# Attention, soft MoE and Mish MLP on one core: the attention order written out for all five queues, the values' products in two blocks a pair

## The chip, the cores and the metric

The kernel runs on 1 core of one Trainium2 chip. The metric is the device time of one execution in microseconds. The engines are TensorE (PE; its weight loads are listed as PEld), VectorE (DVE), ScalarE (ACT), GpSimd (POOL) and SyncE (SP); here SP issues every DMA transfer. A queue of an engine runs its instructions strictly in the order in which they were put there.

## The reference

Three layers in a row, all inputs float32 but the last layer's weights, which are float64 and are converted on the chip.

```python
def _attn_ref(q, k, v):                       # 4 batches, 8 heads, 576 rows, 64 wide
    q_rot, k_rot = rotate(q), rotate(k)       # rotary embedding
    scores = q_rot @ k_rot.T / sqrt(64)
    attn = exp(scores - max(scores)); attn /= sum(attn) + 1e-9
    return attn @ v

def _moe_ref(x, phi, w1, w2):                 # x: 2304 x 512, 32 slots, 8 experts
    logits = x @ phi
    d = softmax over rows (axis 0); c = softmax over slots (axis 1)
    slot_input = d.T @ x
    slot_out = per expert: relu(slot_input @ w1) @ w2
    return c @ slot_out

def _moe2_ref(x, w_in, w_out):                # 512 -> 2048 -> 512
    h = x @ w_in
    return (h * tanh(softplus(h))) @ w_out
```

## The kernel before, in words

**Attention** works on 16 pairs of heads (`p` = 0 to 15, four pairs a batch). Each of q and k is loaded (`load_pair`), rotated on POOL (`rope_pair`, four tensor operations in `rotate`, L228 to L236), transposed on PE (`f_main`, L285) and split into a high and a low part (ACT L290, DVE L294). Twelve SBUF-to-SBUF transfers (`stack`, L317) lay the parts of both heads out so that three float32r products can stand for one float32 product. The last 64 rows of each head are a remainder and go through `load_rem`, `rope_rem` and `f_rem` once a batch or pair.

A pair has nine score tiles (`S`): four of 128 query rows for each head and one (`s_mm2`, L353) for both heads' remainder rows. Each tile is 4 matmuls of 288 columns (8 in the ninth). `M` is its maximum on DVE (L361), `E` its exponential on ACT (L367). `T`, `K` and `R` transpose the probabilities on PE (L374, L388, L394, L396) and copy them to SBUF (`evac`, L410 or L413, on ACT or DVE by a table or by load counters). `V` (`av(p, 0, c)`, 256 columns) and `W` (`av(p, 1, c)`, 320 columns) multiply them with the values (L429): for each of five blocks of keys `c` one matmul per head, the two heads in the two halves of the array's columns, accumulated in one PSUM tile. Each such matmul is two records in the trace. `X` (`xback`) transposes the result back (L449, L451), takes the routing logits (L455, L457) and scales both by the softmax sums. After every fourth pair a batch goes through five units `m_lt`, `m_cols`, `m_disp`, `m_slots`, `m_rows` (action `F`).

Beside this, 20 pieces of the float64 weights are converted in attention (action `C`: `cv_more`, `cv_act` L500 and L501 on ACT, `cv_bits` L506 to L508 on DVE, `cv_sum` L512 and L513 on POOL, then a store to a scratch in DRAM), and 1 MB weight tiles of the MoE layer are fetched into a ring (`fetch`).

**What sets the order.** `PLAN` is a list of nine steps of one pair, and the loop over `p` emits the actions in that order. The emitted order is a priority: the scheduler that places the instructions on the queues moves them by its own estimate of when each is ready, and only instructions passed to `tc.keep_in_program_order` keep their place among each other. Before, these are the weight fetches, the loads of the first two pairs and the warm-up matmuls. So the five blocks of `V` and of `W`, and the two heads in one block, can be parted by other PE work.

PSUM has eight banks: two tiles of two banks for scores (`ps_s`), three of one bank for everything else (`ps_m`) and one for the values' products (`ps_a`).

**After attention** (from `m_sit`, L778) come the experts (`h_ps` L834, `so_ps` L900), which read the ring of weight tiles, and the Mish MLP (`hp` L1004, `o_ps` L1038), which is most of the time from 440 us on.

Of the kernel before, what the change touches and what calls it, by code (L numbers as in the profile page):

```python
# [7 lines left out]
F32 = mybir.dt.float32  # L8
# [13 lines left out]
QA, QAR, QZ, QBR, QB, KC, QKW = 0, 512, 576, 640, 704, 1216, 2432  # L22
# [15 lines left out]

EVAC = {"T3": "d", "T4": "d", "K1": "a", "T0": "a", "T5": "a", "T2": "a"}
# [3 lines left out]
def kernel(  # L43
# [30 lines left out]
    ps_m = psx.enter_context(tc.tile_pool(name="ps_m", bufs=3, space=PSUM))  # L74
    ps_a = psx.enter_context(tc.tile_pool(name="ps_a", bufs=1, space=PSUM))
# [105 lines left out]
    load = {"a": 0.0, "d": 0.0}  # L181
# [73 lines left out]
    part = {}  # L255

    def f_rem(p):
        if p >= NP:
            return
        b, hp = divmod(p, H // 2)  # L260
        ps = ps_m.tile([128, 2, 1, R], F32, tag="m", name="m_rem")
        nc.tensor.transpose(ps.rearrange("p a o r -> p (a o r)"), rem[b][:, hp * 128:(hp + 1) * 128], ident)
        for x in "hl":
            part[x, p] = ae.tile([128, 2, 640], F32R, tag="part" + x, name="part" + x)
        src = ps.to_broadcast([128, 2, 2, R])
        hi, lo = (part[x, p].rearrange("p a (o r) -> p a o r", r=R)[:, :, 0:10:9, :] for x in "hl")

        def act():
            nc.scalar.copy(hi, src)
            load["a"] += 270  # L270

        def dve():
            nc.vector.tensor_tensor(out=lo, in0=src, in1=hi.bitcast(F32), op=ALU.subtract)
            load["d"] += 330

        act_q.append(act)
        dve_q.append(dve)

    def f_main(p, nm):
        if p >= NP:  # L280
            return
        ps = ps_m.tile([128, 512], F32, tag="m", name="m_" + nm)
        t = rope.pop((nm, p))
        for c in range(4):
            nc.tensor.transpose(ps[:, c * 128:(c + 1) * 128], t[:, c, :], ident)  # L285
        i, scale = ("qk".index(nm), SCALE if nm == "q" else 1.0)
        hi, lo = (part[x, p][:, i, R:R + 512] for x in "hl")

        def act():
            nc.scalar.activation(out=hi, in_=ps, func=AF.Copy, scale=scale)  # L290
            load["a"] += 480

        def dve():
            nc.vector.scalar_tensor_tensor(out=lo, in0=ps, scalar=scale, in1=hi.bitcast(F32),  # L294
                                           op0=ALU.mult, op1=ALU.subtract)
            load["d"] += 600
            if p:
                for h in range(2):
                    stack(p, nm, h)

        act_q.append(act)
        dve_q.append(dve)

    def stack(p, nm, h):

        st, s2 = qk_st[p % 2], k2_st[p % 2]
        for x, o in (("h", 0), ("l", 64)):
            t = part[x, p][64 * h:64 * h + 64]
            if nm == "q":
                c = (QA, QBR)[h]  # L310
                todo = [(st[o:o + 64, c:c + S], t[:, 0, R - h * R:][:, 0:S])]
# [3 lines left out]
            for out, in_ in todo:  # L315
                if p or h:
                    nc.sync.dma_start(out=out.bitcast(F32), in_=in_.bitcast(F32))  # L317
                else:

                    (nc.vector.tensor_copy if o else nc.scalar.copy)(out, in_)  # L320

    act_q = []
    dve_q = []

    def flush(lst):
        while lst:
            lst.pop(0)()

    def s_mm(p, s, qc, h, first, last):
        st = qk_st[p % 2]  # L330
        for half in range(2):
            o = h * S + half * 288
            nc.tensor.matmul(s[:, half, 0:288], lhsT=st[:, qc:qc + 128], rhs=st[:, KC + o:KC + o + 288],  # L333
                             start=first, stop=False)
            nc.tensor.matmul(s[:, half, 0:288], lhsT=st[:, qc:qc + 128], rhs=k2_st[p % 2][:, o:o + 288],  # L335
                             start=False, stop=last)

    def s_tile(p, t, h):

        s = ps_s.tile([128, 2, 512], F32, tag="s", name="s")  # L340
        if t < 4:
            s_mm(p, s, (QA, QB)[h] + t * 128, h, True, True)
        else:
            s_mm2(p, s)
        return s

    def s_mm2(p, s):
        st = qk_st[p % 2]
        for half in range(2):
            n = 0  # L350
            for o, qc in ((half * 288, QAR), (KB + half * 288, QZ)):
                for rhs in (st[:, KC + o:KC + o + 288], k2_st[p % 2][:, o:o + 288]):
                    nc.tensor.matmul(s[:, half, 0:288], lhsT=st[:, qc:qc + 128], rhs=rhs,  # L353
# [800 lines left out]
```

## Time and profile before

| | us |
|---|---|
| median of 3 runs | 674.24 |
| lowest and highest of them | 671.77, 676.41 |
| span of the profiled execution | 670.1 |
| first score matmul in it | 19.33 |
| remainder tile (L353) of pair 1 and of pair 15 | 59.64, 378.50 |
| `m_sit`, first work after attention | 397.35 |

The span runs from the first to the last instruction; the median also holds what lies around it, 4.1 us here. Busy time of PE is the union of its instructions with modelled ends, so the chain of waits is used for the length of a single piece.

### The profile page before, as it was taken

To read this page: it belongs to the slowest core of one execution; us is meant where nothing else is said; L and a number is where in the kernel's file an instruction comes from. 1 tells how busy PE (TensorE), PEld (TensorE's weight loads), DVE (VectorE), ACT (ScalarE), POOL (GpSimd) and SP (SyncE) were. 2 spreads that over 40 slices of the span, in tenths; PEclk is the share of its full clock that TensorE was granted. 3 is DMA by queue.
4 is the path that set the end of the run, shared out by engine and by line. 5 is a ranking of instruction groups with operands and counts; after the bars stand their busy time and mean duration, and the time that the engine had idled before them with its cause. 6 is when DMAs were issued, how large, how long until landed. Compare 5 with 4: busy or idle time off the path is not lost.

```text
span 670.1 us, 11089 instructions
## 1 busy us (share of the span) xinstructions
PE 625.2 (93%) x4022; PEld 461.3 (69%) x4022; DVE 406.5 (61%) x824; ACT 336.4 (50%) x757; POOL 218.2 (33%) x263
## 2 busy tenths in 40 slices
PE   1598999989899999999999998999999999999997
PEld 1475677666577767777667653377787888888885
DVE  5777888786686866565756533177876533353342
ACT  2566776684776556665656411167765312222121
POOL 5758869755858644345400010000000000000000
PEclk9999999999999999999999999999999999999999
DMA  9678689868786965346359499962400200030004
GB/s 259 160 187 236 187 268 273 231 212 237 161 266 218 264 184 166 103 128 189 81 176 302 158 338 324 389 262 95 156 33 31 64 1 0 1 95 0 1 1 94
DMA packets 59607, 109.43 MB, mean 163 GB/s; under 512 B 12832, under 2 KB 25248, under 8 KB 59040
## 3 DMA queue, kind: packets, MB, share of 16 engines
q1 hardware_dynamic: 59552, 108.72, 54.2%
q8 instruction: 32, 0.52, 0.3%
q14 instruction: 23, 0.19, 0.1%
HBM read 70.25 MB, written 9.96 MB: 120 GB/s over the span
## 4 chain that ended last, share of the span: by engine, by line
PE 77%; DMA 9%; DVE 7%; ACT 2%; POOL 2%; issue 2%; SPq 1%; DVEq 0%; ACTq 0%; POOLq 0%
PE o_ps L1038 29%; PE m_av L429 13%; PE t L374 7%; PE s L333 5%; PE s L335 4%; PE hp L1004 3%; PE s L353 2%; DMA w<-in_moe_w_in_dram 2%; PE so_ps L900 2%; DMA w<-in_moe_w_dram 2%; DVE nmax L361 1%; PE m_lg L455 1%; PE tk L388 1%; PE m_k L285 1%; DMA w<-in_moe_w_out_dram 1%
## 5 line engine op out<-in xcount | busy, mean ns | idle before, releaser
L361 DVE TENSOR_REDUCE nmax<-s 128x1 f32<-128x576 f32 x144 | 108.0, 753 | 64.3 <-PE s L335 39.5
L367 ACT ACTIVATE P<-s,nmax 128x576 f32<-128x576 f32 x144 | 107.2, 745 | 36.3 <-DVE nmax L361 25.5
L1038 PE MATMUL o_ps<-wo_l,gh 128*128 128x512 f32 x288 | 112.9, 392 | 0.0
L1038 PE MATMUL o_ps<-wo_h,gh 128*128 128x512 f32 x288 | 112.9, 392 | 0.0
L1038 PE MATMUL o_ps<-wo_h,gl 128*128 128x512 f32 x288 | 100.7, 390 | 0.9 <-DVE gl L1019 0.9
L1011 ACT ACTIVATE room<-hp 128x512 f32<-128x512 f32 x72 | 43.0, 599 | 106.7 <-PE hp L1004 102.2
L333 PE MATMUL s<-qk_st 128*128 128x288 f32 x256 | 85.6, 349 | 10.3 <-ACT P L367 5.2
L374 PE MATMUL t<-cs,P 128*128 128x128 f32 x512 | 79.0, 282 | 4.8 <-ACT P L367 2.7
L410 ACT COPY PT<-t 128x512 f32<-128x512 f32 x92 | 53.5, 586 | 49.8 <-PE t L374 49.2
L429 PE MATMUL m_av<-PT,w 128*64 128x320 f32 (+1 forms) x384 | 73.3, 421 | 1.9 <-ACT PT L399 1.3
L374 PEld LDWEIGHTS t<-cs,P 128*128 128x128 f32 x512 | 59.6, 143 | 21.8 <-issue 9.7
L335 PE MATMUL s<-k_st,qk_st 128*128 128x288 f32 x256 | 73.8, 302 | 0.0
L333 PEld LDWEIGHTS s<-qk_st 128*128 128x128 f32 x256 | 49.9, 195 | 29.5 <-ACT P L367 9.1
L1013 DVE CAST gh<-room 128x512 fp32r<-128x512 f32 x49 | 20.9, 427 | 79.4 <-ACT room L1011 79.3
L1038 PEld LDWEIGHTS o_ps<-wo_h,gl 128*128 128x128 f32 x288 | 53.9, 188 | 13.2 <-DVE gl L1019 1.7
L231 POOL TENSOR_TENSOR w<-w,cs 128x512 f32<-128x512 f32 x34 | 45.2, 1332 | 54.1 <-PE m_k L285 46.6
L1038 PEld LDWEIGHTS o_ps<-wo_h,gh 128*128 128x128 f32 x288 | 54.1, 188 | 9.4
L1038 PEld LDWEIGHTS o_ps<-wo_l,gh 128*128 128x128 f32 x288 | 54.3, 189 | 9.0 <-DVE wo_l L891 0.2
L1019 DVE TENSOR_TENSOR gl<-room,gh 128x512 fp32r<-128x512 f32 x72 | 49.6, 691 | 4.6
L335 PEld LDWEIGHTS s<-k_st,qk_st 128*128 128x128 f32 x256 | 50.2, 196 | 0.0
L228 POOL TENSOR_TENSOR w<-w,cs 128x512 f32<-128x512 f32 x34 | 45.7, 1345 | 8.6 <-DMA w<-in_q_dram 2.9
L429 PEld LDWEIGHTS m_av<-PT,w 128*64 128x64 f32 x384 | 26.5, 136 | 23.0 <-issue 9.2
(175 smaller groups left out, 1011.5 us busy)
## 6 DMA issues: line engine op xcount, KB each, us to landing
w<-in_moe_w_dram SPq DMA_DIRECT2D x28, 1024.0 KB, 7.1
w<-in_moe_w_in_dram SPq DMA_DIRECT2D x16, 512.0 KB, 7.3
qk_st<-parth SPq DMA_DIRECT2D x46, 144.0 KB, 3.2
qk_st<-partl SPq DMA_DIRECT2D x46, 144.0 KB, 3.2
room<-in_moe_w_out_dram SPq DMA_DIRECT2D x12, 512.0 KB, 3.6
w<-in_q_dram SPq DMA_DIRECT2D x16, 256.0 KB, 5.2
w<-in_k_dram SPq DMA_DIRECT2D x16, 256.0 KB, 4.6
w<-in_moe_w_dram SPq DMA_DIRECT2D x16, 256.0 KB, 5.6
```

The lines of the kernel that those rows point to most:

```text
L228: eng.tensor_tensor(out=tb, in0=src, in1=sin.to_broadcast([128, n, w]), op=ALU.mult)
L231: eng.tensor_tensor(out=dst, in0=sv, in1=cv, op=ALU.mult)
L333: nc.tensor.matmul(s[:, half, 0:288], lhsT=st[:, qc:qc + 128], rhs=st[:, KC + o:KC + o + 288], start=first, stop=False)
L335: nc.tensor.matmul(s[:, half, 0:288], lhsT=st[:, qc:qc + 128], rhs=k2_st[p % 2][:, o:o + 288], start=False, stop=last)
L361: nc.vector.tensor_reduce(out=stat[p][0][:, i:i + 1], in_=s[:, :, 0:288], axis=AX.XY, op=ALU.max, negate=True)
L367: nc.scalar.activation(out=P[p, t][:, h * S:(h + 1) * S].rearrange("p (a b) -> p a b", a=2), in_=s[:, :, 0:288], func=AF.Exp, bias=stat[p] ...
L374: nc.tensor.transpose(ps[:, j, :], P[p, t][:, blk * 128:(blk + 1) * 128], ident)
L410: nc.scalar.copy(dst, src)
L429: nc.tensor.matmul(ps[o:o + 64, :], lhsT=lhsT, rhs=rhs, start=(c == 0), stop=(c == 4))
L1011: pin(nc.scalar.activation(out=gg, in_=hp, func=AF.Mish))
L1019: pin(nc.vector.tensor_tensor(out=gl, in0=gg, in1=gh.bitcast(F32), op=ALU.subtract))
L1038: pin(nc.tensor.matmul(ops[i, n], lhsT=g_[:, cols], rhs=w_[f], start=(j == 0 and (x, k) == (0, 0)), stop=(j == NG - 1 and all(y[0] != n fo ...
```

## The change

`PLAN` becomes one flat list of some 110 steps that a steady period runs through, each with a lag: a step `name@n` in period `t` works on pair `t - n`. Every engine is wrapped in `InOrder`, which passes each instruction of attention to `tc.keep_in_program_order`; so PE, ACT, DVE, POOL and SP each run exactly the listed order. The old functions are cut into one function per engine and step.

- `A0` to `A4` (256 columns) and `B0@1` to `B4@1` (320 columns) are the values' products. Steps between them in the list (`la`, `z0`, `E2`, `E3` and so on) are work of other engines, so on PE each five stand together. `ps_a` is gone, `ps_m` has four banks, and the products take their bank from it.
- Conversions start with pair 1 (`CV0 = 1`) with two pieces a period: `ci` load, `Ca` ACT, `Cb` DVE, `Cs` POOL, `co` store.
- `wf@2` holds one weight fetch per period at its place, for `p` = 2 to 9, so in periods 4 to 11. The later fetches follow named last uses (`LAST_SCRATCH`, `LAST_ROPE`, `LAST_EARLY`, `LAST_V`), which fall into periods 14 and 15.
- `load_vrem`, the remainder values' loads, is taken out of `load_rem` and issued two pairs later.
- Before the loop, the loads of pair 1 stand behind the stacking transfers of pair 0. `Hk@-1`, the transposes of pair 1's k, stand on PE ahead of pair 0's first score.
- PT copies `t5` and `t7` are on DVE, all other `t`, `k` and all `x` copies on ACT. The remainder rows of the two heads swap places in the stacked q (`QAR`, `QBR`), and the third transpose and the third logits product of a pair are 128 wide instead of 64.

```diff
-    "L T7- S M K1- E V3- V4-",
...
-    "V0 K0 T5 d C F S F M T6 V1 E X1- d V2",
+    "S0 y0@1 Cs0@1 E8@1 ropek@-1 hka t5@1 M0 Z@2 ci0 T6@1 hkd S1 R@1 zz@2 K1@1 ropeR@-1 co0@1 dk "
+    "M1 t6@1 E0 rA@1 rD@1 E1 X0@1 k1@1 w0@1 ca0@1 T7@1 S2 t7@1 Ca1@1 Hq Q@1 M2 S3 M3 qD@1 hqa "
+    "wf@2 Cb1@1 qA@1 B0@1 E2 B1@1 E3 B2@1 B3@1 B4@1 D@1 S4 z1@1 x1@1 hqd Ca0 Cs1@1 T3 M4 X1@1 dq "
+    "t3 w1@1 T0 S5 dD@1 M5 Y1@1 t0 y1@1 Cb0 co1@1 dA@1 lv@1 ca1@1 T2 T1 E4 t2 S6 K0 T4 M6 ci1 E5 "
+    "lC@1 t1 La S7 Lb ra k0 G@-1 t4 E6 A0 la z0 A1 lb ropeq@-1 A2 rb rc M7 A3 lA A4 x0 ga@-1 lB "
+    "S8 ld@-2 gd@-1 T5 E7 M8 Y0 Hk@-1 "
...
-    ps_m = psx.enter_context(tc.tile_pool(name="ps_m", bufs=3, space=PSUM))
-    ps_a = psx.enter_context(tc.tile_pool(name="ps_a", bufs=1, space=PSUM))
+    ps_m = psx.enter_context(tc.tile_pool(name="ps_m", bufs=4, space=PSUM))
+    class InOrder:
+        def __getattr__(self, name):
+            f = getattr(self.engine, name)
+            return lambda *a, **k: tc.keep_in_program_order(f(*a, **k))
+    pe, act, dve, pool_, sp = (InOrder(e) for e in (nc.tensor, nc.scalar, nc.vector, nc.gpsimd, nc.sync))
...
+    dma = sp.dma_start
...
+    def load_vrem(b):
         vv = v[b, :, 512:S, :].rearrange("(g two) s d -> two s g d", two=2)
...
-            av_ps[p, g] = ps_a.tile([128, n], F32, tag="av", name="m_av")
+            m_ps["av", p, g] = ps_m.tile([128, 256 + g * R], F32, tag="m", name="m_av")
...
-            if g and p + 3 < NP:
-                load_v(p + 3)
+    def x_copy(p, g):
+        xs = xts[p, g] = a4.tile([128, 256 + g * R], F32, tag="xts", name="xts")
+        act.copy(xs, m_ps.pop(("av", p, g)))
+    def blocks(xs, g):
+        return [xs[:, o:o + 128] for o in (0, 128, 192)[:2 + g]]
...
     load_pair(1)
     load_v(1)
-    rope_pair(1, "k", nc.gpsimd)
-    rope_pair(1, "q", nc.gpsimd)
-    behind.append(True)
...
+    def loads(p):
+        if 1 <= p < NP - 2:
+            load_pair(p + 2)
+        if p % (H // 2) == 1 and p // (H // 2) + 1 < NB:
+            load_rem(p // (H // 2) + 1)
+        if p % (H // 2) == 3 and p // (H // 2) + 1 < NB:
+            load_vrem(p // (H // 2) + 1)
...
+             "ld": loads, "lv": lambda p: load_v(p + 3) if p + 3 < NP else None,
+             "wf": lambda p: fetch(ahead.pop(0), behind=True) if 2 <= p < 2 + NRA else None,
...
+    for period in range(first, NP + last):
+        for name, n in plan:
+            p = period - n
+            if 0 <= p < NP:
+                steps[name](p)
+                after(name, p)
```

In the list `S`, `M`, `E`, `T`, `K`, `R` are as before (`t`, `k` the copies, `Q` the remainder's last transpose, `rD`, `rA`, `qD`, `qA` its copies). `Hk`, `Hq`, `G` are the next pair's transposes, `hka`, `hkd`, `hqa`, `hqd`, `ga`, `gd` its parts on ACT and DVE, `dk`, `dq` its stacking transfers. `x`, `X`, `Y`, `z`, `y`, `w`, `ca` are the pieces of `xback`. `ld` loads q and k, `lv` values. `La` to `lC`, `D`, `dD`, `dA`, `Z`, `zz`, `ra`, `rb`, `rc` are the batch's units.

## Rows read from the trace of the kernel before

**Rows 1.** The page, busy us (share of the span) xinstructions of each engine.
```profile
PE 625.2 (93%) x4022; PEld 461.3 (69%) x4022; DVE 406.5 (61%) x824; ACT 336.4 (50%) x757; POOL 218.2 (33%) x263
```

**Rows 2.** Table by stretches: busy us of each engine, granted clock, DMA share, GB/s.
```profile
core 0: us, PE busy (x) PEld busy (x) DVE busy (x) ACT busy (x) POOL busy (x), PEclk, DMA share, GB/s
74.00:210.00 136.00, 129.67 (x894) 93.31 (x894) 105.28 (x214) 93.24 (x222) 98.77 (x115) 0.99 0.82 235
244.00:346.00 102.00, 101.64 (x715) 71.71 (x713) 63.18 (x146) 61.72 (x155) 41.34 (x61) 1.00 0.56 154
124.00:134.00 10.00, 10.00 (x73) 7.34 (x72) 7.84 (x17) 5.47 (x14) 8.38 (x8) 1.00 1.00 258
420.00:430.00 10.00, 10.00 (x128) 3.79 (x124) 1.83 (x4) 2.02 (x4) 0.00 (x0) 1.00 1.05 382
```

**Rows 3.** Chain of waits through one pair, 268.70 to 290.46: start, us, what.
```profile
264.19 0.44 PE t L374 x4
...
268.70 1.26 PE s L353 x8
...
271.17 0.58 PE m_av L429 x4
271.75 0.33 PE s L333
272.08 0.13 PE s L335
...
279.54 1.77 PE m_av L429 x12
...
283.70 0.68 PE m_av L429 x2
284.38 0.59 PE t L374 x4
...
289.01 1.45 PE m_av L429 x12
290.46 1.25 PE s L353 x8
```

**Rows 4.** Chain of waits over the whole span, single pieces.
```profile
158.82 7.77 DMA w<-in_moe_w_in_dram
...
378.50 1.25 PE s L353 x8
...
384.57 3.33 PE m_av L429 x20
...
397.35 1.04 PE m_sit L778 x8
```

**Rows 5.** Waits of SP's queue and of ACT (us, times, longest); a DMA issue line.
```profile
SPq L188 <- PE m_av L429: 95.1, 14, 12.2
...
ACT w L500 <- DMA w<-in_moe_w_in_dram: 7.5, 7, 2.4
ACT w L500 <- DMA w<-in_moe_w_out_dram: 3.4, 1, 3.4
...
w<-in_moe_w_in_dram SPq DMA_DIRECT2D x16, 512.0 KB, 7.3
```

**Rows 6.** Groups on POOL in 74:346: xcount | busy us, mean ns | idle before.
```profile
L231 POOL TENSOR_TENSOR w<-w,cs 128x512 f32<-128x512 f32 x26 | 35.0, 1347 | 49.2 <-PE m_k L285 43.8 <-PE m_rem L262 4.0 <-DVE w L507 1.1
```

**Rows 7.** Timeline of the start: SP's issues, PE's first scores of pairs 0 and 1.
```profile
6.07 0.47 SPq L188 DMA_DIRECT2D w<-in_q_dram  x1
...
14.97 0.53 SPq L317 DMA_DIRECT2D qk_st<-parth  x1
...
19.33 0.58 PE L333 MATMUL s<-qk_st 128*128 128x288 f32 x1 [4.17 <-DVE qk_st L320]
...
44.28 0.38 PE L333 MATMUL s<-qk_st 128*128 128x288 f32 x1
59.64 0.40 PE L353 MATMUL s<-qk_st 128*128 128x288 f32 x1 [1.40 <-ACT P L367]
```

More of the change, by code (lines that the diff above doesn't have):

```diff
@@ L255 @@
     part = {}
[L257 to L262, printed above, removed]
-        for x in "hl":
[L264 to L283, printed above, removed]
-        for c in range(4):
[L285 to L302, printed above, removed]
+    m_ps = {}
@@ L316, in stack, with s_mm @@
                 if p or h:
-                    nc.sync.dma_start(out=out.bitcast(F32), in_=in_.bitcast(F32))
+                    dma(out=out.bitcast(F32), in_=in_.bitcast(F32))
                 else:
[L320 to L329, printed above, removed]
+                    (dve.tensor_copy if o else act.copy)(out, in_)
+    def s_mm(p, s, qc, h):
         st = qk_st[p % 2]
@@ L332, in s_mm @@
             o = h * S + half * 288
[L333 to L345, printed above, removed]
+            pe.matmul(s[:, half, 0:288], lhsT=st[:, qc:qc + 128], rhs=st[:, KC + o:KC + o + 288],
+                      start=True, stop=False)
+            pe.matmul(s[:, half, 0:288], lhsT=st[:, qc:qc + 128], rhs=k2_st[p % 2][:, o:o + 288],
+                      start=False, stop=True)
     def s_mm2(p, s):
@@ new lines, in t_head, with pt_of, out_of @@
+    def t_head(p, i):
+        t, h = divmod(i, 2)
+        ps = m_ps["T", p, i] = ps_m.tile([128, 4, 128], F32, tag="m", name="t")
+        for j in range(4):
+            blk = 5 * h + j
+            pe.transpose(ps[:, j, :], P[p, t][:, blk * 128:(blk + 1) * 128], ident)
+    def pt_of(p, g):
+        if (p, g) not in PT:
+            PT[p, g] = (a2, a4)[g].tile([128, 9, 256 + g * R], F32, tag=f"PT{g}", name="PT")
+        return PT[p, g]
+    def out_of(on, dst, src):
+        (act.copy if on == "a" else dve.tensor_copy)(dst, src)
@@ new lines, in blocks, with x_pe, lg_pe @@
+    def blocks(xs, g):
+        return [xs[:, o:o + 128] for o in (0, 128, 192)[:2 + g]]
+    def x_pe(p, g):
+        ps = m_ps["X", p, g] = ps_m.tile([128, 3, 128], F32, tag="m", name="m_x")
+        for j, xb in enumerate(blocks(xts[p, g], g)):
+            pe.transpose(ps[:, j, :], xb, ident)
+    def lg_pe(p, g):
+        lg = m_ps["Y", p, g] = ps_m.tile([128, 3, 2, NSLOT], F32, tag="m", name="m_lg")
+        ph = phi_sb[:, p % (H // 2)].rearrange("p h s -> p (h s)")
+        for j, xb in enumerate(blocks(xts[p, g], g)):
+            pe.matmul(lg[:, j], lhsT=xb, rhs=ph, start=True, stop=True)
@@ new lines, with lt_pe, lt_max @@
+    HALVES = ((0, 512), (512, R))
+    def lt_pe(b, i):
+        o, n = HALVES[i]
+        ps = dmat["s", b, i] = ps_m.tile([NSLOT, 512], F32, tag="m", name="m_lt")
+        for t in range(o // 128, (o + n + 127) // 128):
+            w = min(S - t * 128, 128)
+            pe.transpose(ps[:, t * 128 - o:t * 128 - o + w], c_all[0:w, b, t], ident[0:w, 0:w])
+    def lt_max(b, i):
+        new, nxt = nM[b % 2], nM[(b + 1) % 2]
+        dve.tensor_reduce(out=new[:, i:i + 1], in_=dmat["s", b, i][:, 0:HALVES[i][1]], axis=AX.X, op=ALU.max,
+                          negate=True)
+        if i:
+            dve.tensor_reduce(out=nxt[:, 2:3], in_=new[:, 0:3 if b else 2], axis=AX.X, op=ALU.min)
@@ L681, in one @@
-    def one(lst):
-        if lst:
-            lst.pop(0)()
-    tiles = [(t, h) for t in range(4) for h in range(2)] + [(4, 0)]
-    sc = {}
-    def scores(p, i):
-        sc[p, i] = s_tile(p, *tiles[i])
-    def maxima(p, i):
-        s_max(p, *tiles[i], sc[p, i])
-        load["d"] += 665
-    def expo(p, i):
-        s_exp(p, *tiles[i], sc.pop((p, i)))
-        load["a"] += 717
-    def back(p, g):
-        xback(p, g)
-        b, hp = divmod(p, H // 2)
-        if g and hp == H // 2 - 1:
-            fill.extend(moe_units(b))
@@ L725 @@
[L725 to L738 removed]
+    CV0, NCV = 1, NFB * KDM + NCE
@@ new lines, with after @@
+    for nm in "qk":
+        steps |= {"H" + nm: feeds(main_pe, nm), f"h{nm}a": feeds(main_hi, nm), f"h{nm}d": feeds(main_lo, nm)}
+    for side in range(2):
+        steps |= {f"{n}{side}": conversion(f, side)
+                  for n, f in (("ci", cv_load), ("Ca", cv_act), ("Cb", cv_bits), ("Cs", cv_sum), ("co", cv_store))}
+    plan = [(w.split("@")[0], int((w.split("@") + ["0"])[1])) for w in PLAN]
+    first, last = min(n for _, n in plan), max(n for _, n in plan)
+    def after(name, p):
+        if (name, p) == LAST_SCRATCH:
```

478 lines of the change are left out of this document (256 added, 222 removed).

## The prediction

> **What bounds the kernel now.** I read the page's first two parts, then the table by stretches, then the chain of waits through one pair, then the queue waits and the DMA issues. TensorE (PE) shows as busy for 93% of the span [rows 1], but attention, the part that the change rewrites, is the first 400 us only; from `m_sit` at 397.35 on [rows 4] nothing is edited. In the stretches of attention [rows 2] PE is full (101.64 of 102 us in 244:346, 129.67 of 136 in 74:210), DVE fills 77%, ACT 69%, POOL 73% of the stretch 74:210, and the DMA engines 0.82 of it, 0.56 later. So PE is the bound, with little room behind it in the first half.
>
> The chain [rows 3] shows what fills PE. A pair runs there from one 8-matmul remainder tile (`s` L353) to the next, 268.70 to 290.46: 21.76 us without a gap. The values' products (`m_av`) stand in it in nine places: 0.58, 0.68, 0.68, 1.77, 0.68, 0.68, 0.58, 0.57 and 1.45, together 7.67 us for 40 records (the rows show four of the nine, the first and the last among them). A head of a pair has its own half of the array's columns. Where both heads' products lie side by side (x12, three blocks of keys), a block of keys costs 1.45/3 = 0.48 us at 256 columns and 1.77/3 = 0.59 at 320. Where one head stands alone (x2), it costs 0.68 at 320 columns by itself, more than both together. And the instruction behind each of the nine places is late: the first score matmul takes 0.33 instead of 0.13, a group of four transposes 0.59 instead of 0.44.
>
> Over all pairs, the remainder tile of pair 1 starts at 59.64 and that of pair 15 at 378.50 [rows 4]: 14 periods of 22.78 us. The 1.02 us above the full pair are the token-routing batches of every fourth pair and stalls.
>
> **The change, part by part.** *Products in two blocks.* A0 to A4, and B0 to B4, follow each other on PE, and a helper that pins every instruction keeps both heads of a block of keys together. By the x12 rows the products become 5 x 0.483 + 5 x 0.59 = 5.37 us, 2.30 less. The other bound is the only unbroken run of 20 in the trace, 3.33 us at 320 columns in the tail [rows 4], which has a wait in it; scaled by 1.45/1.77 to 2.73 for the other, the two make 6.06, 1.61 less. I take 2.30: the x12 rows lie in the steady part.
>
> *What follows a block.* Nine late starts (two scores and one remainder tile at 0.19, six others at 0.15) are 1.47 us; two remain, both ahead of scores, 0.38. That is 1.09 less. Of the remainder's third transpose and logits, now 128 wide, nothing comes: a narrow one costs what a wide one does.
>
> Row first, rule second: the late start occurs behind narrow products only [rows 3]. The Trainium skill, "TensorEngine Tiling (Array Packing)", section Tiling Modes (Key Properties), says that a change of tiling mode drains the engine, while different tiles can run at once. By the drain alone the pair would gain the 1.09, by both halves of the rule the 3.39.
>
> A full pair so falls from 21.76 to 18.37 us (19.06 by the other bound); with the 1.02 left as it is, the period would be 19.39.
>
> *One hand order on five queues.* The same instructions, so no engine's work falls but PE's. From 74:210 [rows 2], at 22.8 us a pair, DVE has 17.6 us of work, POOL 16.6, ACT 15.6, the DMA engines 18.7. All fit in 19.39, the DMA engines at 96%. Walking the plan, I find PE's PSUM waits short (four rotating banks, each emptied about two allocations ahead). The tight place is the weight conversion: its load `ci0` is issued near the start of the period and ACT's `Ca0` stands behind the B block. PE's work ahead of that, four score tiles at 0.53, some 20 transposes at 0.11 and B, is about 8 us; such a load lands in 7.3 us at the median [rows 5]. If it is late, the copies and exponentials behind `Ca0` on ACT wait, then PE's `T2`, `T1`, `S6`. The bounds are 0 (plan always ahead) and 3.4 us a period, the longest wait of ACT for such a load [rows 5]. I take 1.0 in the ten periods with conversions, nearer to the mean of its waits (7.5 us in 7), and 0.2 in the four after: 20.4 and 19.6.
>
> Against this the order frees SP: in the kernel before, the next values' load stood ahead of other issues and blocked the queue for 95.1 us in 14 waits, at most 12.2 [rows 5]. In the plan `lv` comes behind the B block that frees its buffer, and `dk` and `dq` leave eight us and more before their scores. Where that stall goes, DMA throughput is next.
>
> *Weight fetches held in place.* One per period, one to two periods later than now, and nine of 1 MB from period 14 on instead of from the end of 13. In 420:430 the engines moved 382 GB/s [rows 2], so nine take 25 us of the two periods and tail, about 50, that remain: covered, no cost. Without cover each costs 2.7 us; I keep 0 to 8 for the last three.
>
> *Start.* Now pair 1's q is issued at 6.07 [rows 7], its k behind it. In the new order they stand on SP behind six stacking transfers of which the first went out at 14.97 [rows 7] and the last, by an estimate from that, at about 18. A load of half the 512 KB that take 7.3 us [rows 5] I put at 4.5, so k of pair 1 lands near 23; POOL rotates it in four operations, two of 1.35 us and two half as wide, some 4.1 us [rows 6], and its transpose (`Hk`) stands ahead of the first score on PE: 27.5 instead of 19.33 [rows 7], 8 us late. But pair 0 now takes from 19.33 to 44.28 [rows 7], with conversions in it, which the plan starts a pair later. Nine tiles and no products, which is what the plan leaves in pair 0's period, I put at 15 us, well under a full 18.37, so pair 1 starts at 42.5. Bounds: 3 us gained to 8 lost; I take 0, pair 1's remainder tile at 59.6. *Later remainder values* take two small transfers from one queue place to another, on a queue that gets shorter waits: 0. Python's load counters cost nothing on the chip.
>
> **The sum.** 59.6 + 10 x 20.4 + 4 x 19.6 = 342.0 for pair 15's remainder tile, against 378.50: 36.5 us less. From there to `m_sit` 18.85 us and from `m_sit` to the end 272.75 stay. The span falls from 670.1 to 633.6. The median of the runs shown, 674.24, lies 4.1 above the span of the profiled execution; with that, 637.7, so **638**.
>
> **The rivals.** *DMA is the next bound.* In the ten periods with conversions the engines reach the 0.82 of 74:210 and no more, so that those periods stay at 22.8 us. For it: waits for transfers are in the chain, 7.77 us at 158.82 [rows 4]. Against it: a single 10-us stretch reaches 1.00 [rows 2], and SP stood blocked. Then 59.6 + 10 x 22.8 + 4 x 19.6 = 366: 662.
>
> *The block gives the drains only* (the change doesn't do what it says: the heads' products don't overlap when all ten stand together). 22.78 - 1.09 + 0.2 = 21.9 a period, 59.6 + 14 x 21.9 = 366: 662. Against it: the x12 rows.
>
> *Head of line on ACT: slower.* A conversion load lands so late that everything pinned behind `Ca0` waits. The gain without stalls is 14 x 3.39 = 47 us, so over ten periods it decides from 4.7 us of stall each, a landing of 12.7 instead of 7.3. At 14 us the stall is 6, 60 in all, 13 more than the gain: 687. For it: full DMA engines, and the 12.2 us that SP once waited. Against it: ACT's longest wait for such a load was 3.4 [rows 5]. The Trainium skill, "TensorE: Matmul & The Clock Gate", opening table, calls ACT's, DVE's and POOL's queues strict first-in first-out, which is the rule behind this rival; the kernel before has fixed queues too, and its ACT waits agree.
>
> **How the numbers follow.** The forecast 0.71, DMA 0.15, drains only 0.05, head of line 0.09. A difference of about 1% is what a measurement of this kernel can tell. The forecast is faster; DMA and drains only are faster by 1.8%, beyond 1% but for 0.03. Of the head of line 0.07 is slower and 0.02 even. Faster 0.88, same 0.05, slower 0.07. The range: with no stalls, 14 x 19.39 gives 331 and 627, with the start's gain and a smaller batch share 618. At the top it takes in DMA and drains only: 664.
>
> **What would show it.** Right: `m_av` in two runs of 20 a pair, 2.4 and 2.9 to 3.3 us long; the remainder tiles 19.5 to 20.5 us apart on the mean; DMA share above 0.88 in the middle; SP's wait for `m_av` gone; first score near 27. Wrong: ACT waits of several us for `in_moe_w_in`, PE waits for ACT behind it, periods of 22.8 us only while conversions run (DMA), or 21.9 throughout (drains only). A first score near 27 with pair 1 not before 50 would put the start's price at its upper end.

## The result and the profile after

The kernel after takes **634.31 us** (median of 4 runs, 631.18 to 634.48) against 675.33 us for the kernel before (4 runs, 671.77 to 677.01). The ratio is 0.9404, with a 95% interval of 0.9356 to 0.9452. The profiled execution has a span of 632.6 us, against 670.1 before. Forecast were 638 us and a span of 633.6.

In the kernel after, one helper records every instruction of attention, so that all of them bear line L83; they are told apart by tiles. First the page's busy line and the table by stretches (columns as in [rows 2]):

```profile
PE 583.3 (92%) x4022; PEld 463.2 (73%) x4022; DVE 416.1 (66%) x807; ACT 339.7 (54%) x774; POOL 221.0 (35%) x263
```
```profile
74.00:210.00 136.00, 127.71 (x1003) 106.18 (x1002) 124.15 (x239) 105.43 (x257) 110.17 (x125) 0.97 0.89 252
82.00:100.00 18.00, 18.00 (x148) 15.12 (x147) 17.06 (x34) 15.54 (x39) 15.82 (x19) 1.00 0.88 235
```

PE does the same 4022 matmuls in 583.3 us where it took 625.2 [rows 1]: 41.9 us less busy time, somewhat more than the 37.5 us by which the span fell. In the stretch 74:210 the share of the DMA engines rose from 0.82 [rows 2] to 0.89. Inside one undisturbed pair, 82:100, PE is full, and VectorE (DVE) with 17.06 of 18 us has become nearly as full; over 74:210 it went from 105.28 [rows 2] to 124.15, with part of that being operations that take longer than before, as shown below. That second engine close behind the first is what the rest of this study is about.

The chain of waits through that pair (start, us, what), to be held against [rows 3]:

```profile
79.24 2.31 PE m_av L83 x20
81.55 1.26 PE s L83 x8
...
88.54 2.84 PE m_av L83 x20
91.38 0.73 PE s L83 x4
...
99.54 1.26 PE s L83 x8
```

The values' products now stand in two runs of 20, 2.31 and 2.84 us, and from one remainder tile to the next (81.55 to 99.54) a pair takes 17.99 us, where it took 21.76. Pair 15's tile starts here:

```profile
341.76 1.28 PE s L83 x8
```

Pair 1's starts at 63.47, so the 14 periods take 19.88 us on the mean, 1.89 more than a full pair: 26.5 us in all. Half of these are waits of PE, and they are few and big. From the timeline of PE (start, us, engine, line, instruction, and in brackets the idle time before it with its releaser), the four of the first half:

```profile
63.47 0.40 PE L83 MATMUL s<-qk_st 128*128 128x288 f32 x1 [1.86 <-ACT P L83]
123.31 0.40 PE L83 MATMUL s<-qk_st 128*128 128x288 f32 x1 [2.17 <-ACT P L83]
142.87 0.40 PE L83 MATMUL s<-qk_st 128*128 128x288 f32 x1 [1.86 <-ACT P L83]
184.71 0.40 PE L83 MATMUL s<-qk_st 128*128 128x288 f32 x1 [1.75 <-DMA w<-in_q_dram]
```

Four more follow: 2.18 at 207.91, 1.86 at 225.91, 0.36 at 269.57 and 1.04 at 288.62. The eight make 13.1 us; the other 13.4 us hold PE's own work for three token-routing batches and whatever a lowered clock adds, which was not separated. Three of the eight are 1.86 us long, four periods apart (periods 1, 5 and 9). The chain of waits that leads to the first of them runs over a DVE operation of the conversion and the maximum behind it to ACT's exponential, for which PE waits:

```profile
57.87 3.03 DVE w L83
...
61.79 0.77 DVE nmax L83
```

The chains of the other two are alike (137.19 and 220.24). Three more of the eight (123.31, 207.91, 288.62) come behind DVE's work for a batch and the short one at 269.57 behind another DVE operation; at 184.71 the releaser is a transfer of q that SP issued at 182.02, by the chain only after a weight fetch of 9.70 us. So seven of the eight, 11.3 us, stand behind DVE. Why that operation is slow is in the timelines of POOL and of DVE, around the first of the 1.86 us waits and around the same step two periods later. POOL:

```profile
57.12 0.74 POOL L83 TENSOR_TENSOR c_all<-tmp 128x64 f32<-128x64 f32 x2 [3.76 <-DVE tmp L83]
57.83 2.51 POOL L83 TENSOR_TENSOR w<-w,cs 128x512 f32<-128x512 f32 x2
...
95.05 1.94 POOL L83 TENSOR_TENSOR c_all<-c_all,tmp 128x64 f32<-128x64 f32 x4 [1.21 <-DVE tmp L83]
...
96.96 2.49 POOL L83 TENSOR_TENSOR w<-w,cs 128x512 f32<-128x512 f32 x2
```

DVE:

```profile
57.86 3.02 DVE L83 SCALAR_TENSOR_TENSOR w<-w,w 128x512 uint32<-128x512 uint32 x1
...
95.72 0.70 DVE L83 SCALAR_TENSOR_TENSOR w<-w,w 128x512 uint32<-128x512 uint32 x1
...
97.59 1.89 DVE L83 TENSOR_SCALAR rz<-z 128x4 f32<-128x4 f32 x1
```

The conversion's bit operation (the second of `Cb0`) takes 0.70 us at 95.72 and 3.02 at 57.86, where POOL began the two 512-wide products of `ropeq` 0.03 us before it. At 95.72 POOL was still in the logits' sum (`ca1`): in a batch's first pair that sum has two additions, 0.74 us, in the others four, 1.94. So only behind the first pair of a batch do POOL's products begin when DVE gets to the bit operation. (In periods 5 and 9 the two recorded starts lie 0.05 and 0.04 us apart the other way, DVE's at 137.19 and 220.24 and POOL's at 137.24 and 220.28; the bit operation takes 3.10 and 3.09 us all the same.) In the other periods of conversions it is a later operation that meets them: the addition of 1e-9 to the softmax sums, 128x4, takes 1.89 us at 97.59, while a like one of 128x5 at 90.95, where POOL had no such product, took 0.16.

How often that happens is in the groups of DVE's instructions in attention (count, busy us, mean ns, idle before), first before (40:345), then after (40:300), with an operation of the batches as the third:

```profile
L507 DVE SCALAR_TENSOR_TENSOR w<-w,w 128x512 uint32<-128x512 uint32 x8 | 5.5, 688 | 0.3 <-DMA scr_in<-w 0.2
L461 DVE TENSOR_SCALAR rz<-z 128x4 f32<-128x4 f32 x13 | 4.5, 345 | 1.1 <-ACT P L367 0.9
L571 DVE TENSOR_TENSOR c_all<-c_all,rst 128x160 f32<-128x160 f32 x3 | 1.0, 319 | 0.1
```
```profile
L83 DVE TENSOR_SCALAR rz<-z 128x4 f32<-128x4 f32 x13 | 14.7, 1131 | 0.0
L83 DVE SCALAR_TENSOR_TENSOR w<-w,w 128x512 uint32<-128x512 uint32 x10 | 14.1, 1408 | 0.4
L83 DVE TENSOR_TENSOR c_all<-c_all,rst 128x160 f32<-128x160 f32 x6 | 7.3, 1218 | 1.0 <-PE m_lt L83 0.7
```

All three were short or mostly short before. After, the bit operation is long in three of its ten periods and the addition in eight of its 13, because the order by hand puts them beside the same POOL products again and again.

The start moved as well. From the chain of the kernel after (start, us, what), to be held against [rows 7]:

```profile
18.68 3.76 DMA w<-in_k_dram
22.57 2.48 POOL w L83 x2
...
27.69 0.97 PE s L83 x4
...
41.31 2.31 PE m_av L83 x20
```

The last line is the A block of pair 0: it stands in pair 0's own period.

And the waits that the prediction spoke of (SP's queue: us, times, longest; then the issues of a conversion load with the median landing), against [rows 5]:

```profile
SPq L83 <- POOL w L83: 47.5, 26, 6.0
...
SPq L148 <- PE m_av L83: 6.0, 1, 6.0
```
```profile
w<-in_moe_w_in_dram SPq DMA_DIRECT2D x16, 512.0 KB, 5.8
```

SP's 95.1 us of waits for `m_av` are 6.0, and ACT's list of waits names no conversion load any more. SP now waits 47.5 us in 26 pieces for POOL to free the pairs' buffers.

### The profile page after: what moved, and what is told of

Same layout as the page of the kernel before. It is cut to its first block, busy times and chain, and to the rows that moved or that the text cites. A ratio compares the mean times of both kernels' runs of the same rounds, so it can differ in the third digit from the quotient of the medians.

```text
span 632.6 us, 11124 instructions
## 1 busy us (share of the span) xinstructions
PE 583.3 (92%) x4022; PEld 463.2 (73%) x4022; DVE 416.1 (66%) x807; ACT 339.7 (54%) x774; POOL 221.0 (35%) x263
## 4 chain that ended last, share of the span: by engine, by line
PE 82%; DVE 8%; DMA 3%; ACT 3%; issue 2%; SPq 1%; POOL 1%; DVEq 0%; ACTq 0%; POOLq 0%
PE o_ps L1087 31%; PE s L83 13%; PE m_av L83 10%; PE t L83 9%; PE hp L1053 3%; DVE w L83 2%; PE h_ps L883 2%; PE so_ps L949 2%; PE m_lg L83 2%; DVE nmax L83 2%; DMA w<-in_moe_w_dram 2%; DMA w<-in_k_dram 1%; ACT P L83 1%; PE m_x L83 1%; PE m_q L83 1%
## 5 line engine op out<-in xcount | busy, mean ns | idle before, releaser
L83 DVE TENSOR_REDUCE nmax<-s 128x1 f32<-128x576 f32 x144 | 107.2, 752 | 37.4 <-PE s L83 35.7
L83 ACT ACTIVATE P<-s,nmax 128x576 f32<-128x576 f32 x144 | 107.3, 746 | 28.4 <-DVE nmax L83 27.5
L83 PE MATMUL s<-qk_st 128*128 128x288 f32 x320 | 105.9, 347 | 14.3 <-ACT P L83 12.5
L83 PE MATMUL s<-k_st,qk_st 128*128 128x288 f32 x320 | 92.2, 303 | 0.0
L83 POOL TENSOR_TENSOR w<-w,cs 128x512 f32<-128x512 f32 x66 | 83.2, 1277 | 23.3 <-DMA w<-in_k_dram 13.1
L83 PE MATMUL t<-cs,P 128*128 128x128 f32 x576 | 87.5, 281 | 0.8 <-ACT P L83 0.4
L83 PEld LDWEIGHTS s<-qk_st 128*128 128x128 f32 x320 | 62.7, 196 | 29.6 <-ACT P L83 18.7
L83 PEld LDWEIGHTS t<-cs,P 128*128 128x128 f32 x576 | 70.8, 146 | 2.0 <-ACT P L83 1.0
L83 ACT COPY PT<-t 128x512 f32<-128x512 f32 (+1 forms) x112 | 61.9, 561 | 17.7 <-PE t L83 16.8
L1087 PEld LDWEIGHTS o_ps<-wo_h,gl 128*128 128x128 f32 x288 | 54.0, 188 | 13.1 <-DVE gl L1068 1.7
L83 PEld LDWEIGHTS s<-k_st,qk_st 128*128 128x128 f32 x320 | 63.2, 197 | 0.0
L83 POOL TENSOR_TENSOR w<-w 128x256 f32<-128x256 f32 (+1 forms) x74 | 59.9, 828 | 3.3
L83 PE MATMUL m_av<-PT,w 128*64 128x320 f32 (+1 forms) x384 | 52.0, 411 | 0.0
L83 POOL TENSOR_TENSOR c_all<-c_all,tmp 128x64 f32<-128x64 f32 (+1 forms) x66 | 25.9, 399 | 50.6 <-DVE tmp L83 48.1
```

The costliest lines, as they stand in the source:

```text
L83: return lambda *a, **k: tc.keep_in_program_order(f(*a, **k))
L1087: pin(nc.tensor.matmul(ops[i, n], lhsT=g_[:, cols], rhs=w_[f], start=(j == 0 and (x, k) == (0, 0)), stop=(j == NG - 1 and all(y[0] != n fo ...
```

## The experiments

All but the last two are the kernel after with one edit. Each time stands beside runs of the kernel before on the same chip: 672.22 for the first four (one run each), 674.02 for the next four (median of 7), 673.03 for the last four (median of 8). As these differ, gains over the kernel after are given by the ratios to before as well, where there are several runs.

**Do the two heads' products overlap?** All five blocks of head 0 are put ahead of those of head 1, at the place of block 4:

```diff
-        if c == 0:
-            m_ps["av", p, g] = ps_m.tile([128, 256 + g * R], F32, tag="m", name="m_av")
+        if c < 4:
+            return
+        m_ps["av", p, g] = ps_m.tile([128, 256 + g * R], F32, tag="m", name="m_av")
...
         for h in range(2):
             o = 64 * h
-            if c < 4:
+            for c in range(5):
...
-            pe.matmul(ps[o:o + 64, :], lhsT=lhsT, rhs=rhs, start=(c == 0), stop=(c == 4))
+                pe.matmul(ps[o:o + 64, :], lhsT=lhsT, rhs=rhs, start=(c == 0), stop=(c == 4))
```

> Each block of the values' products keeps its place and its ten products, but all five of head 0 come first, then all five of head 1, so that two neighbours use the same half of the array. If the price lies in the overlap of the two halves (theory), a lone head's block of keys costs what both cost together, about 0.43 to 0.48 us at 256 columns: the blocks of 2.31 and 2.84 us become about 4.5 and 5.5, a pair gains 4.5 to 5 us and the kernel comes to about 634 + 15 x 4.8 = 705 us. If only the switches of the array's mode cost (rival), the number of switches is the same and the time stays at 634.

Measured: 664.83 us. The chain, a pair of the middle:

```profile
82.39 3.65 PE m_av L83 x20
...
93.05 4.51 PE m_av L83 x20
```

The same 20 products take 3.65 and 4.51 us instead of 2.31 and 2.84: 3.01 us a pair, and the pair goes from 17.99 to 21.0. So the overlap is there, and the rival that only the switches cost is out; but it divides the time by 1.58, not by 2, and the 4.5 to 5 us a pair and 705 us that I expected were too much. Over 14 periods 3.01 would be 42 us and the time rose by 30.5. With a longer pair on PE the other engines have more room: PE's waits between the remainder tiles of pair 1 and pair 15 are 4.6 us in this run's timeline instead of 13.1, which gives back 8.5 of the 11.6 us between.

**Is the unbroken run worth more than the overlap?** The A block is cut in three again, with a transpose and the remainder's scores between:

```diff
-    "lC@1 t1 La S7 Lb ra k0 G@-1 t4 E6 A0 la z0 A1 lb ropeq@-1 A2 rb rc M7 A3 lA A4 x0 ga@-1 lB "
-    "S8 ld@-2 gd@-1 T5 E7 M8 Y0 Hk@-1 "
+    "lC@1 t1 La S7 Lb ra k0 G@-1 t4 E6 A0 la z0 T5 A1 lb ropeq@-1 A2 rb rc M7 A3 lA S8 A4 x0 ga@-1 lB "
+    "ld@-2 gd@-1 E7 M8 Y0 Hk@-1 "
```

> The first block is cut into three places on PE (one block of keys, transposes, three, the remainder tile, one); heads stay side by side. Theory: each of the two added places costs a late start of itself and of its follower, 0.1 + 0.15 us, so 0.5 a pair and 7 to 8 us in all where PE is full: 640 to 642. Rival, that a switch costs nothing and all of the gain is overlap: 634. What stands behind the cut on PE moves with it, so 1 us either way is not read.

Measured: 660.01 us, a miss. The chain of one pair:

```profile
79.91 0.58 PE m_av L83 x4
80.49 0.59 PE t L83 x4
81.07 1.45 PE m_av L83 x12
82.52 1.24 PE s L83 x8
83.76 0.61 PE m_av L83 x4
...
84.44 0.38 ACT xts L83
...
84.87 0.66 PE m_lg L83 x4
```

The pieces are 0.58 + 1.45 + 0.61 = 2.64 instead of 2.31, and the transposes behind the first take 0.59 instead of 0.44: 0.48 us, as expected. But `S8`, moved ahead of `A4`, no longer stands between the block and the logits, and these now wait for ACT's copy of the products at 84.44, 0.53 us in every full pair (a pair takes 19.68 us, 82.52 to 102.20). In the batches PE waits for ACT 2.46 to 3.14 us at transposes (123.71, 212.67, 300.14) where the kernel after has at most 0.16. The edit took away a cover besides cutting the block, so the time does not price the cut.

**What does the pinning give?** First the helper that pins each instruction returns it unpinned, so that the list is only the order of recording; then PE alone is pinned:

```diff
-            return lambda *a, **k: tc.keep_in_program_order(f(*a, **k))
+            return f
```
```diff
-            return lambda *a, **k: tc.keep_in_program_order(f(*a, **k))
+            return (lambda *a, **k: tc.keep_in_program_order(f(*a, **k))) if self.engine is nc.tensor else f
```

> The new emitted order and lags, but no instruction of attention is held in it: the scheduler places all of them by its own estimate. Theory (the order by hand is what keeps the blocks whole): the products fall into several places again, pairs of 20 to 22 us, 650 to 670. Rival (the finer steps and the lags do it, and the scheduler would keep the blocks whole anyway): 634, within 4.

> Only PE's instructions are held in the listed order; ACT, DVE, POOL and SP are placed by the scheduler. Theory: the gain is PE's, so at most a few us are lost, 634 to 640. Rival (the order on the other four queues is what feeds PE in time, SP's above all): PE waits return and it is 650 or more.

Measured: 660.95 without pins, 650.82 with PE alone. Without pins the products are scattered over several places again (119.57 x16, 122.99 x4 in the chain) and `m_sit` starts here, against 360.14 in the kernel after:

```profile
386.74 1.04 PE m_sit L827 x8
```

With PE alone pinned its blocks are whole, 2.31 and 2.84, but PE stands behind engines that work in an order of their own, as its timeline shows:

```profile
65.07 0.71 PE L83 MATMUL m_lg<-phi_sb,xts 128*128 128x64 f32 x4 [3.25 <-ACT xts L428]
```

Here my expectation fell: I had thought PE's order was all. Of the 26.6 us between no pins and all pins, 10 come with PE's pins and 16.5 with those of the other four queues, in this order of adding them; the other order wasn't run, and these are single runs. One thing that the other pins spare is in ACT's list of waits of the kernel with PE alone pinned:

```profile
ACT w L499 <- DMA w<-in_moe_w_in_dram: 12.4, 9, 4.1
```

The scheduler puts ACT's conversion work ahead of copies that PE needs, and ACT stands there for the load; the chain to PE's wait at 65.07 begins with such a load, 7.30 us from 54.40. That is the prediction's head-of-line rival, in a kernel with another order on ACT. The kernel after has no such wait. How much of the 16.5 us it makes was not separated.

**What does the late load of pair 1 cost?** It is issued right behind the first values' load, as early as in the kernel before:

```diff
     load_v(0)
+    load_pair(1)
     rope_pair(0, "k", nc.vector)
...
         stack(0, "q", h)
-    load_pair(1)
     load_v(1)
```

> The loads of pair 1's q and k are put ahead of pair 0's stacking transfers, right behind the first values' load. Theory (the prediction's start): POOL can rotate pair 1's k while pair 0 is prepared, the transposes ahead of the first score no longer wait, the first score falls from 27.69 to about 20 and pair 1's first from 46.14 to 39 to 41, so 627 to 629. Rival (pair 0's own chain of maxima, exponentials and the next pair's q sets when pair 1 starts): the first score is early, pair 1's is not, 633 to 634.

Measured: 628.95 us (628.08 to 630.88), ratio to before 0.9333 (0.9291 to 0.9376), as expected. PE's timeline, the first score of pair 0, of pair 1, and pair 1's remainder tile:

```profile
20.28 0.58 PE L83 MATMUL s<-qk_st 128*128 128x288 f32 x1 [2.17 <-DVE qk_st L83]
...
39.13 0.40 PE L83 MATMUL s<-qk_st 128*128 128x288 f32 x1 [1.31 <-ACT P L83]
57.13 0.40 PE L83 MATMUL s<-qk_st 128*128 128x288 f32 x1 [1.86 <-ACT P L83]
```

The first score comes 7.41 us earlier, pair 1's remainder tile 6.34; the median gains 5.4, by the ratios 4.8. The intervals of the two ratios still overlap at the edge (0.9356 to 0.9376), so by the times alone the gain is not clear of noise; the timeline shows where it comes from. The 1.86 us wait stays.

**Which DVE work makes the stalls?** Three guesses, one edit each. The softmax sums without the added 1e-9 (left out of the computation); POOL's low words of the conversion left out; and the rotation of the remainder moved behind that of q:

```diff
-        dve.tensor_scalar_add(rz[:, i:i + n], z[:, i:i + n], 1e-9)
-        dve.reciprocal(rz[:, i:i + n], rz[:, i:i + n])
+        dve.reciprocal(rz[:, i:i + n], z[:, i:i + n])
```
```diff
-        low_word(pool_, t, sg, w)
+        pass
```
```diff
-    "S0 y0@1 Cs0@1 E8@1 ropek@-1 hka t5@1 M0 Z@2 ci0 T6@1 hkd S1 R@1 zz@2 K1@1 ropeR@-1 co0@1 dk "
+    "S0 y0@1 Cs0@1 E8@1 ropek@-1 hka t5@1 M0 Z@2 ci0 T6@1 hkd S1 R@1 zz@2 K1@1 co0@1 dk "
...
-    "lC@1 t1 La S7 Lb ra k0 G@-1 t4 E6 A0 la z0 A1 lb ropeq@-1 A2 rb rc M7 A3 lA A4 x0 ga@-1 lB "
+    "lC@1 t1 La S7 Lb ra k0 G@-1 t4 E6 A0 la z0 A1 lb ropeq@-1 ropeR@-1 A2 rb rc M7 A3 lA A4 x0 ga@-1 lB "
```

> Leaves out the addition of 1e-9 to the attention's softmax sums, two DVE instructions a pair (a sum is at least 1, so no bit of the result hangs on it). Theory (DVE is the second bound where PE waits, and an SBUF-to-SBUF operation of DVE is held up by POOL's): 32 instructions of 0.16 us that grew to 1.1 to 1.9 us where POOL was at work, so 2 to 5 us less, 629 to 632. Rival (DVE has slack): 634.

> Leaves out POOL's two operations of each weight conversion (the low words are not added), 5.1 of POOL's 16 us a period; loads, ACT's and DVE's parts and the stores stay. Theory (POOL running late holds up DVE's conversion operation for 2.5 us in the three periods with a remainder's rotation, and PE's waits of 1.86 us at 63, 143 and 226 follow from it): those waits and the 3.0-us DVE operation vanish, 8 to 10 us less, 624 to 626. Rival (the waits come from ACT or from transfers): 632 to 635.

> The remainder's rotation (four POOL operations in periods 1, 5 and 9) moves behind the rotation of q. Theory: q's rotation is then no longer late in those periods and does not meet DVE's conversion operation, so three stalls of 2 us with the slow clock behind them go, 626 to 630. Rival: POOL has no room, the delay moves into the next period and meets other DVE work, 633 to 638.

Measured: 627.51 (625.82 to 631.31; ratio 0.9316, 0.9266 to 0.9366) without the addition; 631.33 in a single run without POOL's sum; 633.80 (632.48 to 634.84; ratio 0.9406, 0.9358 to 0.9455) with the remainder's rotation late. The first is right in kind, and the gain is larger than the 2 to 5 us expected, 6.8 by the medians and 5.9 by the ratios, whose intervals again overlap at the edge: the 1.9 us operations are gone, and PE's waits between the remainder tiles of pair 1 and pair 15 fall from 13.1 to 8.9 us, though the three behind the bit operation stay (1.86, 2.00, 2.01). The other two theories fell. The time without POOL's sum lies between theory and rival, but the long operation is still there in both, and so are three waits of 1.86 or 1.87 us (timelines of DVE, first without POOL's sum, then with the late rotation).

```profile
57.75 3.04 DVE L83 SCALAR_TENSOR_TENSOR w<-w,w 128x512 uint32<-128x512 uint32 x1
```
```profile
56.64 3.02 DVE L83 SCALAR_TENSOR_TENSOR w<-w,w 128x512 uint32<-128x512 uint32 x1
```

Neither the conversion's sum on POOL nor the remainder's rotation is what it meets. That left q's products.

**The two parts priced at nothing.** The remainder values' loads go back to the batch's other remainder loads; and the weight fetch (the MoE layer's tiles, not the conversions' weights as the expectation calls it) goes to the end of the order, its lag taken away:

```diff
         rem_raw[b] = t
-
-    def load_vrem(b):
         vv = v[b, :, 512:S, :].rearrange("(g two) s d -> two s g d", two=2)
...
-        if p % (H // 2) == 3 and p // (H // 2) + 1 < NB:
-            load_vrem(p // (H // 2) + 1)
```
```diff
-    "wf@2 Cb1@1 qA@1 B0@1 E2 B1@1 E3 B2@1 B3@1 B4@1 D@1 S4 z1@1 x1@1 hqd Ca0 Cs1@1 T3 M4 X1@1 dq "
+    "Cb1@1 qA@1 B0@1 E2 B1@1 E3 B2@1 B3@1 B4@1 D@1 S4 z1@1 x1@1 hqd Ca0 Cs1@1 T3 M4 X1@1 dq "
...
-    "S8 ld@-2 gd@-1 T5 E7 M8 Y0 Hk@-1 "
+    "S8 ld@-2 gd@-1 T5 E7 M8 Y0 Hk@-1 wf "
```

> The remainder values' loads go back beside the other remainder loads of the batch, a pair earlier in SP's queue, while everything else stays as in the kernel after. Theory (the prediction's: moving them later costs nothing and spares a wait): put early, they want the buffer that the previous batch's last pair has not read yet, SP stands for it, and what is behind them in SP's queue lands later; 640 to 650 us, with SP's waits on m_av above 20 us where the kernel after shows 6.0. Rival: DMA is the only thing that counts and has slack here, 632 to 636.

> The fetch of the conversions' weights is issued at the end of each pair's order instead of the place where it is now held. Theory (the prediction priced the fetch's place at nothing): 631 to 638 us. Rival: its place decides when the next pair's loads land, and the first scores of several pairs come over 1 us later; 645 to 655.

Measured: 634.88 us (633.50 to 636.75; ratio 0.9441, 0.9415 to 0.9466) and 630.96 (629.98 to 634.41; ratio 0.9393, 0.9360 to 0.9427). Both intervals overlap that of the kernel after: neither place is worth anything that can be told. With the fetch at the end, PE's wait at 184.71 is gone, but others of 2.24 and 0.99 us for ACT have come (114.90, 196.13).

With the remainder values my theory of a wait fell, and for a reason that the plan shows: the early loads are listed in the period of a batch's last pair, ahead of that pair's B block (`B4@1`, one period on), so no wait can arise; in this kernel the B blocks of pairs 3 and 7 are computed with the remainder values of two batches later. SP's wait for `m_av` is the same single 6.0 us. So the later place is what lets pinned B blocks find their values; its price in time is nothing that shows. Whether a version that waits for the block would be slower wasn't tried.

**A version that mends what was found.** Pair 1's loads early and no added 1e-9 together; then the same with the bit operation ahead of the second output copy:

```diff
-    "t3 w1@1 T0 S5 dD@1 M5 Y1@1 t0 y1@1 Cb0 co1@1 dA@1 lv@1 ca1@1 T2 T1 E4 t2 S6 K0 T4 M6 ci1 E5 "
+    "t3 w1@1 T0 S5 dD@1 M5 Y1@1 t0 Cb0 y1@1 co1@1 dA@1 lv@1 ca1@1 T2 T1 E4 t2 S6 K0 T4 M6 ci1 E5 "
```

> Pair 1's loads issued right after the first values' loads, and the addition of 1e-9 to the softmax sums left out, together. Theory (one saves at the start, the other in the pairs, so the gains add: 5.4 and 6.8 us off 634.3): 620 to 624 us. Rival (both only shift the same wait for VectorE): 627 to 629.

> As x11_both (the 1e-9 left out here too), and the conversion's second VectorE block, Cb0, listed ahead of the second output copy, so that it runs before GpSimd begins the rotation. Theory (the 3.0 us bit operation is held by GpSimd's products of 512 beside it, and PE's three waits of 1.86 us with the low granted clock behind them follow from it): those operations take 0.7 us, the three waits go, 612 to 617 us. Rival (the output copy then comes late and PE's transposes wait for its bank each period, 0.5 us or more): 622 us or slower, with 0.7 us operations all the same.

Measured: 622.63 us (621.22 to 627.69; ratio 0.9270, 0.9228 to 0.9313), so the two gains add up, within the noise, and together they are clear of the kernel after's interval; and **617.25 us** (615.57 to 620.38; ratio 0.9182, 0.9152 to 0.9213), 17 below the kernel after by the medians, 15 by the ratios. The move alone gives 5.4 on the same chip, and the intervals don't overlap; the median is just above the 612 to 617 that I expected. DVE's timeline of the first around the place, and then POOL's and DVE's of the second:

```profile
51.70 3.02 DVE L83 SCALAR_TENSOR_TENSOR w<-w,w 128x512 uint32<-128x512 uint32 x1
```
```profile
52.65 0.53 POOL L83 TENSOR_TENSOR c_all<-tmp 128x64 f32<-128x64 f32 x2 [5.76 <-DVE tmp L83]
53.14 2.50 POOL L83 TENSOR_TENSOR w<-w,cs 128x512 f32<-128x512 f32 x2
```
```profile
51.22 0.69 DVE L83 SCALAR_TENSOR_TENSOR w<-w,w 128x512 uint32<-128x512 uint32 x1
...
53.65 0.18 DVE L83 RECIPROCAL rz<-z 128x4 f32<-128x4 f32 x1
```

The same operation, ahead of POOL's products, takes 0.69 us, and in all ten periods so: the group's mean fell to 693 ns. PE's waits of 1.87 to 2.01 us in periods 1, 5 and 9 of the first kernel are gone, and so is its wait for a transfer of q at 179.47; from pair 1's remainder tile to pair 15's, PE's waits make 5.6 us instead of 11.1. The first three were the test; why the last went with them was not separated.

## Why the prediction was right, and where only its sum was

**The products.** Forecast 5.37 us a pair and 2.30 less; measured 2.31 + 2.84 = 5.15, 2.52 less. The x12 rows were the right ones to take; the tail's 3.33 was not the price of a block. The head-by-head kernel shows that the gain is overlap, 3.01 us a pair: the rival of the drains only, at 662, is out.

**What follows a block.** Forecast 1.09; of the pair's 21.76 - 17.99 = 3.77 us, 3.77 - 2.52 = 1.25 are left for it and all else. The pair's chain has two late starts, as forecast: the score tile behind B takes 0.73 instead of 0.54, the remainder tile behind A 1.26.

**The hand order's stalls.** This step failed, although its sum came out. The prediction put 1.0 us a period on ACT's `Ca0`, behind a conversion load that lands late, 10 x 1.0 + 4 x 0.2 = 10.8 us in all. ACT's list has no such wait; those loads land in 5.8 us at the median instead of 7.3. Instead PE waits 13.1 us in eight places, 11.3 of them in seven behind DVE. I had counted DVE's work at 17.6 us of a period of 19.39 and called it a fit, by the durations in the kernel before; the order by hand changed the durations, as the groups show. The 1.02 us a period that I left for batches and stalls, 14.3 in all, stands against the 13.4 that the waits leave, so the two terms together were 25.1 over a full pair and came to 26.5.

What makes DVE late is shown by the last kernel for the bit operation and by the one without the addition for the other. For the batches' operations (1218 ns on the mean instead of 319) it was not tested; they are still 1422 ns in the last kernel. The rule is in the Trainium skill, "SBUF — State Buffer", section "Who interferes with whom": a DVE instruction with two inputs in SBUF, or one in a mode that uses both ports, shares a path with GpSimd (POOL); who issues first has it for its whole instruction, and the other stands. The trace agrees that the other stands, with one addition: DVE's operation at 57.86 ended at 60.88, behind both of POOL's products (57.83 + 2.51 = 60.34), so it stood for two instructions in a row. Which of the two came first isn't settled by starts 0.03 to 0.05 us apart, and whether the addition runs in a mode that uses both ports no trace shows.

**The other rivals.** DMA as the next bound is out: the share went to 0.89 where the rival had 0.82, and the pair took 17.99 us with conversions running. The head of line on ACT is out: no wait for such a load in this order; the kernel with PE alone pinned has it.

**SP's wait.** Forecast gone, measured 95.1 to 6.0. Right. **The fetches and the later remainder values** at 0: right within the noise, by the two kernels that move them back.

**The start.** First score forecast 27.5, measured 27.69. Pair 0, though, was put at 15 us, "well under a full 18.37", and takes 18.45 (27.69 to 46.14); with the load early it takes 18.85 (20.28 to 39.13). The step that failed is the 15, and with it its premise: "nine tiles and no products" is not what the plan leaves in pair 0's period. Only `B0` to `B4` lag by one; `A0` to `A4` run in the pair's own period, 2.31 us at 41.31. The timeline shows two more things that the 15 left out: PE waits 0.75 and 0.45 us for ACT's exponentials, and up to about 39 us PE's work comes at some half of its later pace (a score tile in 0.96 us instead of 0.54), as it did at the start of the kernel before. So pair 1's first score stands at 46.14 instead of 42.5, and its remainder tile at 63.47 against 59.6: 3.9 us, inside the bounds of -3 to +8.

**The sum.** Pair 15's remainder tile was forecast at 342.0 and came at 341.76: 3.9 us lost at the start, and 14 periods of 19.88 instead of 20.17 gave 4.1 back. From there to `m_sit` it is 18.38 (18.85 forecast), and the rest 272.46 (272.75). Of the 4.1 the shorter full pair gave some 5.3 (17.99 instead of 18.37) and the rest some 0.9, while the waits took 2.3 more than forecast. The span is right to 1.0 us by two terms that were each off by 4: that they cancel is luck, since nothing ties pair 0's length to a full pair's. The median was forecast at 638, 3.7 too high: besides the 1.0 of the span, the 4.1 us added to it were too many. They set a median against the span of one execution, 670.1, which by its length belongs to the fastest of those runs (671.77); the profiled execution after has 634.42 with a span of 632.6, 1.8 apart.

## What to carry to other kernels

When an order is fixed by hand, walk it for pairs of engines too, not only for each engine's sum of work: an operation of DVE on SBUF beside a long one of POOL can take several times its usual time, and a fixed order makes them meet in every period. A block of products for two heads that lie in different columns is priced from the longest undisturbed run in the steady part of the old trace (here 12 records), and its order keeps all of its gain only if the queues that feed it are pinned with it (650.82 against 634.31 here). Look at the first periods by themselves: write out from the lags what such a period really holds, and take its pace from the start of the old trace, not from its middle.

## What the runs showed of the hardware that was not expected

- DVE's two-input bit operation (128x512) went from 0.69 to 3.02 us, and a 128x4 addition from 0.16 to 1.89, beside POOL's 512-wide products. The bit operation stood through two of them in a row (57.86 to 60.88). A reciprocal of the same 128x4 took 0.18 beside them (53.65 in the last kernel).
- The granted clock was below the full 2.4 GHz in some stretches with waits of PE, and not in others. In the table by stretches of the kernel after (last three columns: clock, DMA share, GB/s), 123:127 follows a wait of 2.17 us, 225:229 begins with the last 0.91 us of one of 1.86, and 143:147 follows one of 1.86 too:

```profile
123.00:127.00 4.00, 3.69 (x19) 3.68 (x20) 3.26 (x6) 3.28 (x10) 3.84 (x5) 0.65 0.57 182
143.00:147.00 4.00, 4.00 (x36) 3.00 (x40) 3.80 (x9) 2.50 (x7) 3.87 (x4) 1.00 0.76 204
...
225.00:229.00 4.00, 3.09 (x16) 3.08 (x17) 3.93 (x7) 2.09 (x6) 3.52 (x3) 0.70 1.05 294
```

  A mean between 0.5 and 1 is a stretch that ran partly at 1.2 GHz. The last kernel, whose longest wait after the start is 1.57 us, had 1.000 over its span (its other runs 1.000, 1.000 and 0.994), the kernel after 0.992. Why one wait is followed by the low level and another isn't was not settled.
- Twenty products for two heads in separate column halves run 1.58 times as fast side by side as one head after the other (2.31 against 3.65, 2.84 against 4.51 us), not twice.
- In pair 0 the matmuls of a score tile follow each other every 0.24 us until about 39 us and every 0.13 after it, while the table lists a granted clock of 1.00 for 27.69:39.20 as for the time behind it. What slows them was not settled.
